# Nine sequence rows per partition, channel projection in the mode domain, and 8 KB weight runs in a linear-attention and spectral-mixing kernel

## The chip, the core and the metric

The kernel runs on one core of one Trainium2 chip. The metric is the device time of one execution in microseconds (us). Times are medians of three to seven executions. The profiler's span of one execution is about 2 us shorter than the time of the same execution.

Engine names as in the profile: PE multiplies matrices, PEld is its weight load, DVE is VectorE, ACT is ScalarE, POOL is GpSimd, SP only issues DMAs here. Casting loads (fp32 in memory, 16 bits on chip) are issued by POOL.

## The reference, cut to what matters

```python
# q, k, v: (8 batches, 8 heads, 576 rows, 64), w_r, w_i: (64 modes, 512, 512), w_ch: (512, 512), all fp32
phi = lambda x: np.where(x > 0, x, np.exp(x) - 1.0) + 1.0
kv  = einsum('bhsd,bhse->bhde', phi(k), v);  z = phi(k).sum(axis=2)
x   = einsum('bhsd,bhde->bhse', phi(q), kv) / (einsum('bhsd,bhd->bhs', phi(q), z)[..., None] + 1e-6)
x   = x.transpose(0, 2, 1, 3).reshape(8, 576, 512)
X   = rfft(x, axis=1)                       # only the first 64 modes are mixed
Yr  = Xr @ w_r - Xi @ w_i;  Yi = Xr @ w_i + Xi @ w_r      # per mode, 16 rows x 512 x 512
u   = x + irfft(Y, n=576)
out = u + maximum(u @ w_ch, 0)
```

The spectral weights are 128 matrices of 1 MB in fp32, 134 MB of the 164 MB that the kernel reads. Reading them cannot be avoided, so everything else should happen under it.

## The kernel before

Attention runs batch by batch. Seven weight buffers are filled while it runs. Then one mode after another is multiplied as its two matrices arrive. Results of four modes sit in four bands of 32 partitions, so a later stage has to bring them into one tile per batch. This is done by DMAs of 8 KB. The inverse DFT, the channel product and the output come last.

```python
def _w_load(kk):                                        # seven buffers; 2 KB runs: row (dc*128 + p) of the matrix
    wr = wpool.tile([128, NDC, D], BF16, tag="w", bufs=7)
    nc.gpsimd.dma_start(out=wr, in_=moe_w_r[kk].rearrange("(dc p) e -> p dc e", p=128))
    ...                                                 # the same for wi
for b in range(B):                                      # attention
    if b % 2 == 0: w_pref[b // 2] = _w_load(b // 2)
    for c in range(2):                                  # 512 B runs of q, k; 256 B runs of v; 64 tail rows apart
        nc.gpsimd.dma_start(out=q16[:, c], in_=q[b, :, c*256:(c+1)*256, :].rearrange("h (s2 par) d -> s2 h (par d)", par=2))
        ...
    ...
    nc.vector.tensor_copy(out=xt_c[:, :, 0, b, :], in_=xt_ps)       # DFT of x, transposed, modes contiguous
    ...
for g in range(NG):                                     # 16 groups of four modes
    for m in range(4):
        ...                                             # 4 matmuls with wr, 4 with wi, all into band mo = 32*m
    for m in range(4):
        nc.vector.tensor_copy(out=ystage[mo:mo+16, gg, :], in_=p1[mo:mo+16, :])
    if gg == HNG - 1:                                   # twice: 64 DMAs that reorder lanes into batches
        for b in range(B):
            for ri in range(2):
                for m in range(4):
                    nc.sync.dma_start(out=yg[b][k0+8*m : k0+8*m+8, ri, :], in_=ystage[lane : lane+1, :, :])
for b in range(B):                                      # output, per tile of 128 rows
    for j in range(NB + 1):
        ...                                             # 2 matmuls: inverse DFT; DVE: u = x + y
        nc.scalar.copy(out=u16, in_=u)                  # then 4 transposes, another ACT copy,
        ...                                             # 4 matmuls with w_ch, DVE: u + max(e, 0), store
```

## Time and profile before

The median is 594.36 us (592.34 to 595.3, 3 runs). The stages, as the chain of waits and the stretches below divide them:

| stretch, us | what | what sets its length |
|---|---|---|
| 0 to 174 | attention | 13 to 18 us from the DFT copies of one batch to those of the next, 16.3 on average (the 17.8 of the prediction fits two of these steps); no engine is full |
| 133 to 175, within it | DMA idle | seven buffers are full; the eighth load waits for the first product |
| 174 to 490 | weights | DMA: 2.54 us per 1 MB matrix, PE follows |
| 490 to 535 | reorder | SP issues 64 DMAs at 0.66 us each |
| 535 to 592 | rest of the output | PE 47 of 57 us |

The slice table of the kernel before: each column is 1/40 of the span (14.8 us). Digits are tenths of the time that the engine or the DMA engines were busy; PEclk is the granted PE clock in tenths; GB/s counts the bytes written, which for a casting load are half of those read.

```profile
PE   0378799999855665666666566766666654999885
PEclk9999999655556667666676766566767675857999
DMA  9999998992019999999999999999999990004444
GB/s 159 168 186 182 182 173 74 124 85 24 1 16 193 206 206 206 206 206 207 206 206 206 209 210 210 207 206 206 206 206 206 206 188 10 13 12 164 168 171 142
```

The row of DMA falls to 2, 0, 1 at 133 to 175 us. From there it is 9 in every slice at 206 GB/s until 490 us (206 to 210), then 0 for three slices (10 to 13 GB/s), then 4. The stretches, with the busy time of each engine in us (and its number of instructions), then granted clock, DMA share and GB/s:

```profile
core 0: us, PE busy (x) PEld busy (x) DVE busy (x) ACT busy (x) POOL busy (x), PEclk, DMA share, GB/s
40.00:174.00 134.00, 113.79 (x966) 71.84 (x967) 95.17 (x346) 76.00 (x120) 45.17 (x54) 0.75 1.04 99
174.00:490.00 316.00, 199.91 (x506) 54.27 (x503) 41.21 (x60) 0.00 (x0) 89.63 (x121) 0.66 1.22 203
490.00:535.00 45.00, 37.34 (x132) 11.18 (x130) 26.71 (x40) 11.87 (x21) 0.00 (x0) 0.65 0.07 12
535.00:592.00 57.00, 46.96 (x273) 20.62 (x272) 29.94 (x45) 30.06 (x59) 0.00 (x0) 0.95 0.48 167
```

Two pieces of the chain of waits of the kernel before (start in us, duration in us, what):

```profile
144.76 29.38 issue
174.15 5.37 DMA wi_1715<-in_moe_w_i_dram
179.52 17.86 DMA wi_2332<-in_moe_w_i_dram
...
493.63 0.71 DVE ystage_2740 L336
495.00 0.62 SPq L345
495.67 0.62 SPq L345
```

POOL issues nothing for 29.4 us because no buffer is free. In the list of waits it is this line (engine, line, releaser: us in total, times, longest):

```profile
POOL wi_1715 L120 <- PE P_0_2268 L317: 29.4, 1, 29.4
```

From 495 us on the chain is one SP issue of 0.62 us after the other, 0.66 us apart with the gap.

### The profile page before, as it was taken

The page shows a single profiled execution, that of the slowest core. Times are in us where ns is not written, and L with a number is a line of the kernel's source. Part 1 is how long each engine was busy: PE and PEld are TensorE (multiplying, and loading weights), DVE is VectorE, ACT ScalarE, POOL GpSimd, SP SyncE. Part 2 cuts the span into 40 slices and gives each one's busy share as a digit, 9 for nine tenths or more (in the row PEclk, how much of TensorE's full clock was granted, in tenths as well). Part 3 has the DMA queues.
Part 4 walks back from the last instruction along what each step waited for, and adds up shares of the span by engine and source line. Part 5 has one row for each costly group of instructions (what it writes and reads, how often), then busy time and mean ns, then how long its engine had stood idle before and what let it go on. Part 6 is the DMA issues. An engine that isn't in the chain of part 4 may idle for free.

```text
span 592.1 us, 5577 instructions
## 1 busy us (share of the span) xinstructions
PE 410.4 (69%) x1976; PEld 166.8 (28%) x1976; DVE 209.9 (35%) x529; ACT 131.7 (22%) x218; POOL 158.0 (27%) x205
## 2 busy tenths in 40 slices
PE   0378799999855665666666566766666654999885
PEld 0255465655521111111111111111111111323442
DVE  1486977877511101110110100311011103576653
ACT  1346666764420000000000000000000001602673
POOL 6656444430013323222323322223223200000000
PEclk9999999655556667666676766566767675857999
DMA  9999998992019999999999999999999990004444
GB/s 159 168 186 182 182 173 74 124 85 24 1 16 193 206 206 206 206 206 207 206 206 206 209 210 210 207 206 206 206 206 206 206 188 10 13 12 164 168 171 142
DMA packets 155243, 94.21 MB, mean 159 GB/s; under 512 B 83280, under 2 KB 150480, under 8 KB 155216
## 3 DMA queue, kind: packets, MB, share of 16 engines
q0 software_dynamic: 138896, 80.75, 96.0%
q1 hardware_dynamic: 16320, 13.12, 8.1%
q8 instruction: 15, 0.25, 0.2%
q14 instruction: 12, 0.10, 0.0%
HBM read 164.10 MB, written 9.44 MB: 293 GB/s over the span
## 4 chain that ended last, share of the span: by engine, by line
DMA 55%; PE 20%; issue 11%; SPq 7%; DVE 3%; ACT 2%; POOL 1%; DVEq 0%; POOLq 0%; ACTq 0%
SPq L345 7%; DMA wi_2332<-in_moe_w_i_dram 3%; DMA wr_2872<-in_moe_w_r_dram 3%; DMA wi_2821<-in_moe_w_i_dram 3%; DMA wi_2426<-in_moe_w_i_dram 3%; DMA wi_3009<-in_moe_w_i_dram 3%; DMA wi_2609<-in_moe_w_i_dram 3%; DMA wr_3060<-in_moe_w_r_dram 3%; DMA wr_2477<-in_moe_w_r_dram 3%; DMA wr_2660<-in_moe_w_r_dram 3%; DMA wi_2520<-in_moe_w_i_dram 3%; DMA wr_2966<-in_moe_w_r_dram 3%; DMA wi_2915<-in_moe_w_i_dram 3%; DMA wr_2571<-in_moe_w_r_dram 3%; DMA wi_3151<-in_moe_w_i_dram 3%
## 5 line engine op out<-in xcount | busy, mean ns | idle before, releaser
L370 ACT CAST u_0_0_3240<-x_main_76 128x512 f16<-128x512 f32 x1 | 0.6, 620 | 328.4 <-DVE x_main_76 L368 328.4
L326 PEld LDWEIGHTS <-xt_c 128*16 128x16 bf16 x256 | 32.3, 126 | 136.4 <-issue 132.2
L317 PEld LDWEIGHTS <-xt_c 128*16 128x16 bf16 x256 | 28.7, 117 | 127.9 <-issue 102.2
L336 DVE CAST ystage_2740<-P_8_2741 16x512 bf16<-16x512 f32 x4 | 2.7, 687 | 45.5 <-PE P_10_2847 L326 45.5
L219 PE MATMUL qT_0_146<-id_64,qp_128 128*64 128x128 f16 x8 | 1.3, 314 | 23.8 <-DVE qp_128 L179 23.8
L361 PEld LDWEIGHTS <-inv_sb 64*128 64x128 bf16 (+1 forms) x80 | 7.4, 111 | 28.0 <-issue 23.3
L219 PEld LDWEIGHTS <-qp_128 128*64 128x64 f16 x32 | 3.2, 158 | 25.3 <-DVE qp_128 L179 23.8
L336 DVE CAST ystage_2267<-P_1_2305 16x512 bf16<-16x512 f32 x4 | 2.7, 686 | 19.6 <-PE P_1_2305 L326 19.6
L336 DVE CAST ystage_2740<-P_13_3006 16x512 bf16<-16x512 f32 x4 | 2.7, 686 | 17.9 <-PE P_13_3006 L326 17.9
L336 DVE CAST ystage_2267<-P_7_2623 16x512 bf16<-16x512 f32 x4 | 2.7, 687 | 17.7 <-PE P_7_2623 L326 17.6
L336 DVE CAST ystage_2267<-P_3_2411 16x512 bf16<-16x512 f32 x4 | 2.8, 688 | 17.7 <-PE P_3_2411 L326 17.6
L336 DVE CAST ystage_2267<-P_5_2517 16x512 bf16<-16x512 f32 x4 | 2.7, 687 | 17.7 <-PE P_5_2517 L326 17.6
L336 DVE CAST ystage_2267<-P_6_2570 16x512 bf16<-16x512 f32 x4 | 2.7, 687 | 17.7 <-PE P_6_2570 L326 17.6
L336 DVE CAST ystage_2267<-P_2_2358 16x512 bf16<-16x512 f32 x4 | 2.7, 686 | 17.7 <-PE P_2_2358 L326 17.6
L336 DVE CAST ystage_2740<-P_15_3112 16x512 bf16<-16x512 f32 x4 | 2.8, 688 | 17.6 <-PE P_15_3112 L326 17.6
L336 DVE CAST ystage_2267<-P_4_2464 16x512 bf16<-16x512 f32 x4 | 2.7, 686 | 17.7 <-PE P_4_2464 L326 17.6
L336 DVE CAST ystage_2740<-P_14_3059 16x512 bf16<-16x512 f32 x4 | 2.7, 687 | 17.6 <-PE P_14_3059 L326 17.6
L336 DVE CAST ystage_2740<-P_11_2900 16x512 bf16<-16x512 f32 x4 | 2.7, 686 | 17.6 <-PE P_11_2900 L326 17.6
L336 DVE CAST ystage_2740<-P_12_2953 16x512 bf16<-16x512 f32 x4 | 2.7, 686 | 17.6 <-PE P_12_2953 L326 17.5
L120 POOL DMA_DIRECT2D wi_1715<-in_moe_w_i_dram x1 | 0.8, 756 | 29.4 <-PE P_0_2268 L317 29.4
L336 DVE CAST ystage_2267<-P_0_2268 16x512 bf16<-16x512 f32 x4 | 2.7, 686 | 9.8 <-PE P_0_2268 L326 9.7
L336 DVE CAST ystage_2740<-P_10_2847 16x512 bf16<-16x512 f32 x4 | 2.7, 687 | 9.5 <-PE P_10_2847 L326 9.5
(1543 smaller groups left out, 1070.2 us busy)
## 6 DMA issues: line engine op xcount, KB each, us to landing
wr_105<-in_moe_w_r_dram POOLq DMA_DIRECT2D x1, 512.0 KB, 7.3
wi_107<-in_moe_w_i_dram POOLq DMA_DIRECT2D x1, 512.0 KB, 9.8
q_0_109<-in_q_dram POOLq DMA_DIRECT2D x2, 256.0 KB, 11.8
k_0_110<-in_k_dram POOLq DMA_DIRECT2D x2, 256.0 KB, 12.9
v_0_111<-in_v_dram POOLq DMA_DIRECT2D x4, 128.0 KB, 11.8
q_1_375<-in_q_dram POOLq DMA_DIRECT2D x2, 256.0 KB, 9.3
k_1_376<-in_k_dram POOLq DMA_DIRECT2D x2, 256.0 KB, 9.7
v_1_377<-in_v_dram POOLq DMA_DIRECT2D x4, 128.0 KB, 9.1
```

Source lines behind the costliest of these rows:

```text
L120: nc.gpsimd.dma_start(out=wi, in_=moe_w_i[kk].rearrange("(dc p) e -> p dc e", p=128))
L219: nc.tensor.transpose(qT_ps[po : po + 64, j, :], q_p16[:, c, h, par, :], id16[:, :128])
L317: nc.tensor.matmul(p1[mo : mo + 16, :], xa[:, dc], wr[:, dc, :], start=(dc == 0), stop=False, tile_position=(0, mo),)
L326: nc.tensor.matmul(p1[mo : mo + 16, :], xb[:, dc], wi[:, dc, :], start=False, stop=(dc == NDC - 1), tile_position=(0, mo),)
L336: nc.vector.tensor_copy(out=ystage[mo : mo + 16, gg, :], in_=p1[mo : mo + 16, :])
L345: nc.sync.dma_start(out=yg[b][k0 + 8 * m : k0 + 8 * m + 8, ri, :], in_=ystage[lane : lane + 1, :, :],)
L361: nc.tensor.matmul(yps[:rows, :], inv_sb[:NM, ri, j * 128 : j * 128 + rows], yg[b][:, ri, :], start=(ri == 0), stop=(ri == 1),)
L370: nc.scalar.copy(out=u16[:rows, :], in_=u)
```

## The change

Its intent: (1) each partition takes nine consecutive rows of one head, so q, k and v arrive in runs of 9 x 64 x 4 = 2304 B with no tail rows; (2) the weights arrive with four consecutive matrix rows per partition, in runs of 8 KB; (3) 14 matrices instead of 7 can be loaded early; (4) the four 128-row parts of a product use four column groups of the PE, and their sum, together with the reordering, is done by a matmul with a 0/1 "pick" matrix, so the 128 small DMAs go; (5) u @ w_ch = x @ w_ch + irfft(Y @ w_ch): x @ w_ch is computed under the weight stream, Y @ w_ch on 16 rows per mode, and the output stage only adds.

```diff
-        nc.gpsimd.dma_start(out=wr, in_=moe_w_r[kk].rearrange("(dc p) e -> p dc e", p=128))   # 7 buffers
+            nc.gpsimd.dma_start(out=w, in_=src[kk].rearrange("(p dc) e -> p dc e", dc=NDC))    # 4 + 10 buffers
...
+            nc.gpsimd.dma_start(out=t, in_=src[b].rearrange("h s d -> (h s) d").rearrange(
+                    "(hp r j) d -> r hp (j d)", r=128, j=NJ))                # one load each for k, q, v
+        if b >= 1: ...                                                        # w_load(b - 1): two matrices per batch
...
-                    nc.vector.tensor_copy(out=xt_c[:, :, 0, b, :], in_=xt_ps)  # modes contiguous
+        nc.vector.tensor_copy(out=xt_v[:, :, :, 1, b], in_=xf[:, :, 0, :])     # 24 columns per mode: 48 B stride
+        nc.vector.tensor_copy(out=xt_v[:, :, :, 2, b], in_=xf[:, :, 1, :])
+        nc.scalar.mul(out=xt_v[:, :, :, 0, b], in_=xf[:, :, 1, :], mul=-1.0)
...
+            nc.tensor.matmul(P[quad, :], xt_c[:, dc, 8 + kk*SLOT : 8 + kk*SLOT + 32], wr[:, dc, :],
+                start=True, stop=False, tile_position=(0, dc * 32))             # quad = rows dc*32 .. dc*32+31
...                                                                             # the same with wi and stop=True
+            nc.tensor.matmul(yt_ps[:, ec, kk % 8, :], st[:, ec*128 : ec*128+128], pick_sb)
...
-                        nc.sync.dma_start(out=yg[b][...], in_=ystage[lane : lane + 1, :, :])   # 2 x 64 of them
+        if 4 <= kk < 52: ... channel_product(done)       # 36 tiles: x16, 4 transposes, copy, 4 matmuls, E0
+        if kk == NE - 1: ...                             # mode 55: z = Y @ w_ch and y = Y per batch, 112 of 128 rows
...
+    def finish(t, by_act):                               # output, 36 tiles
+        nc.tensor.matmul(e, id16, E0[t], ...); nc.tensor.matmul(y, inv, Y); nc.tensor.matmul(e, inv, Z, ...)
+        nc.vector.tensor_tensor(out=x, in0=x, in1=y, op=ALU.add)
+        if by_act:                                       # 16 tiles: relu on ACT, add on POOL
+            nc.scalar.activation(out=r, in_=e, func=AF.Relu)
+            nc.gpsimd.tensor_tensor(out=x, in0=x, in1=r, op=ALU.add)
+        else:                                            # 20 tiles: one DVE instruction
+            nc.vector.scalar_tensor_tensor(out=x, in0=e, scalar=0.0, in1=x, op0=ALU.max, op1=ALU.add)
```

## The prediction

> **What bounds it now.** The slice table and the chain of waits show four stages.
> (1) Attention, 0 to 174 us: about 17.8 us per batch (spacing of the DFT matmuls in the chain). No engine is full (18 us windows: PE 15.5, DVE 14, ACT 11).
> (2) At 133 to 175 us the DMA row falls to 2, 0, 1: seven weight buffers are full and the eighth load waits on the weight product (wi_1715, 29.4 us).
> (3) Weights, 175 to 490: the chain is nearly all weight DMA, DMA 9 of 9, 206 GB/s written as bf16, so 412 GB/s read as fp32; one 1 MB matrix per 2.54 us. PE (63%, clock 0.65) only follows.
> (4) 494 to 535: 64 small DMAs issued by SP at 0.66 us each, on the chain; then 57 us of output work with PE 47, DVE 30, ACT 30.
>
> **What the change does.**
> - Stage 4's 64 reorder DMAs vanish (PE picks rows instead; 8 small DMAs stay): about -38 us.
> - During attention 14 weight matrices can load instead of 7. So 114 remain after it: 114 x 2.54 = 290 us; before, 121.
> - 8 KB source runs instead of 2 KB. "DMA: Bandwidth & Descriptors" (Why small descriptors are slow) gives about 3 bus cycles per packet and (Measured) 425 GB/s at best, so at most 3%: estimate 2.47 to 2.54 us per matrix, 282 to 290 us.
> - q, k, v arrive in runs of 2304 B instead of 512 and 256 B, without 64-row tails. Estimate per batch from traced durations (DVE 0.40 per 128x256 multiply, 0.69 per 2048 fp16 scalar op; ACT 1.9 per 2048 exp): DVE 11, ACT 10.6, PE 10 to 12 us. DMA per batch (3.5 MB q,k,v plus 2.1 MB weights) at 412 GB/s: 13.7 us. So attention becomes DMA-paced at 13.5 to 14.5 us per batch, 44 MB by about 109 us; the last v lands then, with some 18 us of work behind it: attention ends near 128 us (118 to 145).
> - The channel product x@w_ch moves under the weight stream. Per mode PE gets 8 matmuls of 512 columns in four column groups, 4 picks, 0.75 channel product: under 3.5 us if the groups overlap ("TensorE: Matmul & The Clock Gate", Part 3), under the 5 us of DMA. All hidden.
> - Output stage: 36 tiles; 36 adds at 0.69 plus 20 relu-adds at 0.69 make DVE 39 us; 108 wide matmuls on PE about 27 to 40; 16 relus on ACT and adds on POOL. DVE-paced, 42 to 46 us.
>
> **Sum.** 128 attention + 4 restart (buffers full: DMA idles 15 to 20 us until mode 2 runs) + 286 stream + 8 last mode, z/y and small DMAs + 45 output = 471; about 2 more from span to time: 473 us. Range 452 to 502. Chances: faster 0.97, same 0.02, slower 0.01.
>
> **What would show it.** Slice table: DMA 9 over nearly all slices, with one gap of 15 to 20 us at the end of attention. Weight landings 2.47 to 2.54 us apart. In the stream, chain = weight DMA, PE under 75%. No SP issue row. Output stage DVE at 85% or more.
>
> **What would make it wrong.** Attention compute-paced (permuted fp16 views at half rate on DVE add 2.4 us per batch; shared PSUM slots stall PE): +15 to 25 us. The column groups not overlapping at a cold clock: PE 5.6 us per mode, stream PE-bound, +30 us. Output stage PE-paced at a half clock: +10 us. 8 KB runs bringing more than 3%: -10 us.

## The result and the profile after

The kernel after takes 487.6 us (486.92 to 488.39, 4 runs); the kernel before took 593.93 us in the same rounds. The ratio is 0.8214 (95% interval 0.819 to 0.8238). Ratios here are the mean time of one kernel's runs over that of the other's of the same rounds, so not quite the ratio of the medians quoted. All outputs were correct, in the experiments too. The time lies in the predicted range and is 14.6 us above the predicted 473.

The slice table of the kernel after (one column is 12.1 us):

```profile
PE   0344576556747675677675433232323359429870
PEclk9957655565557979988979755555555559757996
DMA  9999999990006999999999999999999999962995
GB/s 160 211 209 209 209 211 209 211 209 17 1 0 121 213 214 213 213 214 213 214 213 214 213 214 214 213 213 212 215 212 215 212 215 211 215 124 75 283 274 171
```

The DMAs are full from the start, at about 209 GB/s from the second slice on. Then there is one hole of three slices, and then mostly 213 to 214 GB/s until the last weight. The three slices of 10 to 13 GB/s near the end are gone. The stretches of the kernel after, with the same columns as before:

```profile
20.00:112.00 92.00, 50.61 (x656) 34.86 (x656) 67.73 (x146) 66.74 (x75) 20.00 (x29) 0.59 1.13 206
112.00:149.00 37.00, 21.85 (x240) 13.62 (x242) 18.86 (x41) 16.14 (x19) 0.14 (x1) 0.50 0.00 1
149.00:434.00 285.00, 146.49 (x1084) 65.39 (x1076) 44.02 (x82) 61.71 (x108) 60.42 (x114) 0.70 1.05 210
434.00:442.00 8.00, 5.88 (x23) 2.08 (x20) 1.36 (x3) 1.17 (x2) 0.00 (x0) 0.50 0.08 24
442.00:476.00 34.00, 26.50 (x111) 9.65 (x109) 33.51 (x56) 9.56 (x16) 20.18 (x16) 0.99 0.82 247
476.00:485.00 9.00, 0.00 (x0) 0.00 (x0) 0.00 (x0) 0.00 (x0) 0.00 (x0) 0.56 0.39 127
```

In 112 to 149 us the DMAs move nothing, although the last load of attention has landed and 114 weight matrices are still to come. The chain of waits across this hole:

```profile
97.15 0.35 POOL v_7_1362 L141
97.50 51.34 issue
148.86 0.51 POOL wr_1732 L119
...
160.50 19.13 DMA wr_1889<-in_moe_w_r_dram
```

and the wait of POOL behind it:

```profile
POOL wr_1732 L119 <- PE P_1627 L278: 51.0, 1, 51.0
```

v_7 is the last v. It was issued at 97.15 us and landed at 111.1 us. The next load is the first one that needs a freed weight buffer, and it is issued at 148.86 us. So nearly 38 us of work lay between the last landing and the freed buffer. How the time fell, from the chain and from the landings:

| from, to | before, us | after, us | saved |
|---|---|---|---|
| start to the first load that needs a freed buffer | 174.2 | 148.9 | 25.3 |
| to the landing of the last weight | 315.4 (121 matrices) | 285.0 (114 matrices) | 30.4 |
| to the end of the span | 102.6 | 51.4 | 51.2 |
| span | 592.1 | 485.2 | 106.9 |

Of the 30.4 us, seven fewer matrices at 2.61 us are 18.2, and 114 matrices at 0.107 us less are 12.2. (Here the whole stretch, its start included, is divided by the matrices: 315.4 / 121 = 2.61 and 285.0 / 114 = 2.50 us.)

The last 51.4 us hold a part that none of the stages above names. DVE ends at 475.65 us and the last store lands at 480.52. After that no DMA moves anything, and the trace has one long instruction left: a DRAIN on POOL (with which the program closes an engine), from 473.85 to 484.46 us. In the kernel before, POOL has nothing to do at the end, and its DRAIN (16.3 us) is over at 490 us.

### The profile page after: what moved, and what is told of

Its sections match the earlier page's. It is cut to its first block, busy times and chain, and to the rows that moved or that the text cites. A ratio compares the mean times of both kernels' runs of the same rounds, so it can differ in the third digit from the quotient of the medians.

```text
span 485.2 us, 5542 instructions
## 1 busy us (share of the span) xinstructions
PE 255.5 (53%) x2156; PEld 129.4 (27%) x2156; DVE 171.2 (35%) x337; ACT 163.5 (34%) x227; POOL 108.6 (22%) x173
## 4 chain that ended last, share of the span: by engine, by line
DMA 65%; issue 13%; DVE 8%; PE 7%; ACT 4%; POOL 0%; POOLq 0%; SPq 0%; DVEq 0%
DMA q_3_640<-in_q_dram 4%; DMA wi_3418<-in_moe_w_i_dram 4%; DMA wr_2621<-in_moe_w_r_dram 4%; DMA wr_3283<-in_moe_w_r_dram 4%; DMA wr_3109<-in_moe_w_r_dram 4%; DMA wr_2988<-in_moe_w_r_dram 4%; DMA wr_2865<-in_moe_w_r_dram 4%; DMA wr_2500<-in_moe_w_r_dram 4%; DMA wr_2256<-in_moe_w_r_dram 4%; DMA wr_2133<-in_moe_w_r_dram 4%; DMA wr_2012<-in_moe_w_r_dram 4%; DMA wr_2744<-in_moe_w_r_dram 4%; DMA wr_2377<-in_moe_w_r_dram 4%; DMA wr_1889<-in_moe_w_r_dram 4%; DMA k_5_998<-in_k_dram 4%
## 5 line engine op out<-in xcount | busy, mean ns | idle before, releaser
L284 PEld LDWEIGHTS <-xt_c 128*32 128x32 bf16 x248 | 11.8, 101 | 86.1 <-issue 84.9
L278 PEld LDWEIGHTS <-xt_c 128*32 128x32 bf16 x248 | 9.0, 98 | 44.9 <-issue 17.9
L182 PE MATMUL kvp_121<-vpad_100,ke_108 64*128 64x130 f16 x36 | 2.1, 308 | 15.2 <-DVE vpad_100 L171 15.2
L382 PEld LDWEIGHTS <-YT 128*112 128x112 f16 x32 | 7.7, 288 | 2.7 <-issue 2.2
L441 POOL TENSOR_TENSOR x_main_76<-x_main_76,r_3474 128x512 f32<-128x512 f32 x1 | 1.3, 1267 | 29.6 <-ACT r_3474 L440 29.6
L388 PEld LDWEIGHTS <-YT 128*112 128x112 f16 x32 | 7.5, 294 | 0.5
L182 PEld LDWEIGHTS <-ke_108 64*128 64x128 f16 x36 | 2.0, 141 | 15.1 <-DVE ke_108 L168 12.6
L424 PEld LDWEIGHTS <-inv_sb 128*128 128x128 f16 x32 | 3.2, 100 | 8.7 <-issue 6.6
L419 PEld LDWEIGHTS <-id_64 128*128 128x128 f16 x36 | 3.5, 100 | 6.4 <-issue 2.1
L423 PEld LDWEIGHTS <-inv_sb 128*128 128x128 f16 x32 | 3.3, 102 | 4.8 <-issue 1.7
L163 ACT ACTIVATE ke_108<-k_0_102 128x1152 f16<-128x1152 f16 x2 | 2.2, 1154 | 6.5 <-DMA k_0_102<-in_k_dram 6.5
L254 PE MATMUL xf_254<-fwd_sb,x_0_184 128*128 128x128 f16 x16 | 2.2, 263 | 4.0 <-ACT x_0_184 L248 4.0
L163 ACT ACTIVATE ke_468<-k_2_458 128x1152 f16<-128x1152 f16 x2 | 2.3, 1160 | 5.6 <-DMA k_2_458<-in_k_dram 5.6
L292 ACT CAST ys_3429<-P_3420 128x512 f16<-128x512 f32 x1 | 0.6, 586 | 10.4 <-PE P_3420 L284 10.4
L290 DVE CAST ys_3410<-P_3401 128x512 f16<-128x512 f32 x1 | 0.7, 691 | 9.4 <-PE P_3401 L284 9.4
L163 ACT ACTIVATE ke_828<-k_4_818 128x1152 f16<-128x1152 f16 x2 | 2.7, 1326 | 3.9 <-DMA k_4_818<-in_k_dram 3.9
L290 DVE CAST ys_2810<-P_2801 128x512 f16<-128x512 f32 x1 | 0.7, 692 | 9.1 <-PE P_2801 L284 9.1
L290 DVE CAST ys_3122<-P_3113 128x512 f16<-128x512 f32 x1 | 0.7, 691 | 9.1 <-PE P_3113 L284 9.1
L290 DVE CAST ys_2931<-P_2922 128x512 f16<-128x512 f32 x1 | 0.7, 692 | 9.1 <-PE P_2922 L284 9.1
L290 DVE CAST ys_2687<-P_2678 128x512 f16<-128x512 f32 x1 | 0.7, 691 | 9.1 <-PE P_2678 L284 9.1
## 6 DMA issues: line engine op xcount, KB each, us to landing
v_0_106<-in_v_dram POOLq DMA_DIRECT2D x1, 576.0 KB, 11.5
k_2_458<-in_k_dram POOLq DMA_DIRECT2D x1, 576.0 KB, 14.7
```

Of the source, the lines that this page charges most:

```text
L163: nc.scalar.activation(out=ev[:, c], in_=rv[:, c], func=AF.Exp)
L182: nc.tensor.matmul(kv_ps[:, h2, hpp * 130 : hpp * 130 + 130], kp[rows, hpp, j].rearrange("p o d -> p (o d)"), vp[rows, 2 * hpp : 2 * hpp + ...
L254: nc.tensor.matmul(o, x16[:, jj, dc::NDC], fwd_sb[:, jj, :], start=(jj == 0), stop=False)
L278: nc.tensor.matmul(P[quad, :], xt_c[:, dc, 8 + kk * SLOT : 8 + kk * SLOT + 32], wr[:, dc, :], start=True, stop=False, tile_position=(0, dc ...
L284: nc.tensor.matmul(P[quad, :], xt_c[:, dc, kk * SLOT : kk * SLOT + 32], wi[:, dc, :], start=False, stop=True, tile_position=(0, dc * 32),)
L290: nc.vector.tensor_copy(out=st, in_=P)
```

## The experiments

Twelve kernels were run. Two questions lead them: what sets the hole of 37 us and the pace of attention, and what each part of the change is worth.

| label | kernel and edit | us | ratio to before |
|---|---|---|---|
| e1_xt_layout | after, DFT result stored with contiguous modes | 480.41 | 0.8084 |
| e2_after_2k | after, weights in 2 KB runs | 495.29 | 0.8334 |
| e3_before_8k | before, weights in 8 KB runs | 583.47 | 0.9816 |
| e4_no_prefetch | after, no weight loads written between batches | 487.21 | 0.8201 |
| e4b_tied_late | after, all early weights held until the last v is in | 489.7 | 0.8252 |
| e5b_short_runs | after, q, k, v in 256 B runs, four loads each | 494.6 | 0.8336 |
| e5a_four_loads | after, four loads each, long runs | 482.01 | 0.8131 |
| e6_project_late | after, channel product back in the output stage | 510.26 | 0.859 |
| e8_before_twoq | before, reorder DMAs on SP and ACT | 585.99 | 0.9877 |
| e8b_before_poolq | before, reorder DMAs on SP and POOL | 579.35 | 0.9759 |
| e9_best | after, e1's layout and one early weight tied to each batch | 466.1 | 0.7857 |
| e10_balance | e9 with more output tiles on ACT and POOL | 476.46 | 0.8026 |

By the margin of 2% that the record uses, e8_before_twoq counts as the same as the kernel before (interval 0.9844 to 0.9910) and e3_before_8k as unclear (0.9784 to 0.9849). Both intervals lie below 1, so both are faster, but by little.

### e1_xt_layout: is it the strided copies?

One suspect for the hole was the three copies that store the DFT of a batch. Their instructions write 2-byte elements 48 B apart. The edit stores modes contiguously and lets the PE read its weights with a stride instead:

```diff
-        nc.vector.tensor_copy(out=xt_v[:, :, :, 1, b], in_=xf[:, :, 0, :])
+        nc.vector.tensor_copy(out=xt_v[:, :, 1, b, :], in_=xf[:, :, 0, :])
...
-                P[quad, :], xt_c[:, dc, 8 + kk * SLOT : 8 + kk * SLOT + 32], wr[:, dc, :],
+                P[quad, :], xt_c[:, x0[dc] + 8 : x0[dc] + 40, kk], wr[:, dc, :],
```

> The changed kernel with the spectral operand stored with the modes contiguous, so the three copies per batch that write it are dense again instead of 2-byte writes 48 bytes apart. Theory (attention is paced by its own chain of instructions, and these copies, 1.33 and 1.55 us on VectorE and 1.34 us on ScalarE where I had sized 0.31 to 0.37, stand in it): the copies fall to about 0.3 us, a batch in the loop gets 2 to 2.6 us shorter than 14.7, the first spectral product starts 9 to 14 us before 145 us, time 474 to 479 us. Rival (attention is paced by its loads until the last v lands at 111 us): only the work behind that load gets shorter, 4 to 7 us, time 480 to 484. Second rival (the copies are off the chain): 486 to 489.

It took 480.41 us (479.8 to 481.32), which is in the rival's range. Two of the DVE copies in the kernel after (busy us, mean ns | idle before), in its groups of instructions:

```profile
L261 DVE CAST xt_c<-xf_1514 128x256 bf16<-128x256 f32 x1 | 1.5, 1549 | 0.0
L260 DVE CAST xt_c<-xf_434 128x256 bf16<-128x256 f32 x1 | 1.3, 1334 | 2.3 <-PE xf_434 L257 2.3
```

and the copies of all eight batches in e1_xt_layout:

```profile
L258 DVE CAST xt_c<-xf 128x256 bf16<-128x256 f32 x8 | 3.4, 425 | 22.3 <-PE xf L255 18.2 <-PE kvp L180 4.1
L259 DVE CAST xt_c<-xf 128x256 bf16<-128x256 f32 x8 | 3.3, 415 | 0.0
```

The same 128x256 elements take 0.42 instead of 1.33 to 1.56 us on DVE, and 0.39 instead of 1.34 us on ACT. The batches did not come faster while loads were running: the DFT of the sixth batch was stored at 114.9 us against 114.7. Behind the last load they did: 11.5 and 11.6 us for the last two batches against 13.5 and 12.9, and the first load that needs a freed buffer was issued at 143.23 instead of 148.86 us. So the copies cost time only where no load sets the pace. The granted PE clock was 1.00 in attention in this profile and 0.59 in that of the kernel after. But e9_best below has the same 12.2 us between the first numerators (the attention outputs before the DFT) of its last two batches as e1_xt_layout, with a clock of 0.64 from 20 to 120 us. And the four executions of e1_xt_layout had mean clocks of 0.81, 0.82, 0.70 and 0.71 over the span, and all took 479.8 to 481.3 us. So the clock is not what shortened them.

"SBUF — State Buffer" of the Trainium skill (the note on cachelines, in Door 1: The DMA port swizzle) says that accesses pay when each one goes to a new 16-byte line. This case fits it for writes: 48 B apart, an element took three to four times as long. No other distance was tried, so that the lines are the reason is not shown. The price of the strided read that replaces it is on PEld, 155 to 158 ns per load of 32 columns against 98 to 100 ns with contiguous columns, and there it lies under the weight DMAs.

### e4_no_prefetch and e4b_tied_late: do the weight loads slow attention?

The rival: the 14 weight loads share the DMA engines with q, k and v and delay them. In e4_no_prefetch the loads between the batches were only left out of the loop:

```diff
-        if b >= 1:
+        if False:                                   # the loop behind attention loads all of them
```

> The changed kernel with no weight loaded between the batches: all fourteen early matrices are asked for after the last q, k, v. Theory (attention is paced by its own instructions, and its end leaves the DMA idle for 37 us): the fourteen matrices, 34 us of DMA, fit in the idle stretch at the end of attention, the first product stays near 145 us, time 484 to 492 us. Rival A (loads pace attention, weights among them take their turn): attention ends 8 us or more earlier, time under 480. Rival B (early loading is what saves the time): the stream gets the 34 us back, time 510 to 525 us.

It took 487.21 us, but it did not do what it was for. The order in which loads are issued is decided by the scheduler, and the first weight loads appeared in POOL's order at 27 us, among q, k and v. The run says nothing on the question. e4b_tied_late holds the loads back by data: each buffer first gets one element of the last v, so that its load cannot start earlier.

```diff
+            nc.vector.tensor_copy(out=w[0:1, 0, 0:1], in_=raw["v"][0:1, 0, 0:1])
+            nc.gpsimd.dma_start(out=w, in_=src[kk].rearrange("(p dc) e -> p dc e", dc=NDC))
```

> The changed kernel with the fourteen early weight matrices tied by a one-element copy to the last batch's v, so that the scheduler cannot put them among the q, k, v loads (which it did in the run before). Theory (loads pace attention until the last v lands, weights taking their turn in the queue): with the queue to themselves the batches follow at their own pace, 13.4 us as between the last two; the last batch's numerators start near 120 us instead of 133, the first spectral product near 131 instead of 145, the weights still fit before about 137, time 472 to 480 us. Rival (the engines' own chain paces attention): first product 142 to 146 us, the weights come after it, time 487 to 493 us.

It took 489.7 us (489.52 to 489.83), which is in the rival's range; the first product ran at 138.9 us, between what the two sides expected. Its GB/s row, in slices of 12.2 us:

```profile
GB/s 162 207 208 177 124 108 110 145 2 44 213 214 213 213 214 212 215 213 213 214 214 213 213 214 213 213 214 214 213 214 214 213 214 213 213 141 66 290 272 170
```

From the fourth slice on the DMAs carry q, k, v alone and are not full (108 to 177 GB/s). Still the first numerators of the batches come at 25.5, 40.0, 55.0, 69.7, 84.4, 99.1, 113.8 and 127.2 us, 14.5 to 15.0 us apart and the last 13.4. In the kernel after they come at 25.8, 44.5, 60.1, 76.0, 90.7, 105.3, 120.0 and 133.4 us, 14.6 to 15.9 us apart once running and the last 13.4. So the weight loads cost attention about 6 us, nearly all in the first batches. The engines' own chain of instructions, at 14.7 us, is as slow as that even where the DMAs are not full. And no engine is full there either: from 40.0 to 113.8 us, five batches, DVE is busy 56.6 us, ACT 53.9 and PE 48.4, that is 11.3, 10.8 and 9.7 us per batch of 14.75. The batch takes longer than its busiest engine needs, because the engines wait for one another. The first load that needs a freed buffer came at 142.69 us, but now the 14 early weights had to be read after attention, from 117.45 us on. The gain and the loss cancel: the last weight landed at 436.8 us against 433.8.

### e9_best: both limits at once

If two limits of nearly the same length hold attention, taking away either gains little and taking away both gains more. This kernel has e1's layout. It also ties one early weight to the v of each batch from the second on and eight to the last.

```diff
+    W_AFTER = (0, 1, 1, 1, 1, 1, 1, 8)
...
+        for _ in range(W_AFTER[b]):                # one-element copy from this batch's v, then the load
```

> Both together: dense spectral operand, and one weight matrix tied to the v of each of batches 1 to 6, eight to the last v. Theory (loads pace attention until 111 us, then the copies stand in the chain): batches every 11.5 us as between the last two of the dense run, first spectral product 118 to 126 us, DMA nearly without a gap, time 458 to 470 us. Rival (the two gains are the same gain): 473 to 480 us.

It took 466.1 us (465.61 to 467.15), 21.5 us less than the kernel after and the best of all. The batches come 12 to 14 us apart (numerators at 25.4, 39.3, 52.2, 65.4, 78.2, 90.9, 102.9, 115.1 us), the first load that needs a freed buffer at 127.93 us. Its slices (11.6 us each):

```profile
DMA  9999999927999999999999999999999999944985
GB/s 158 207 209 209 209 185 179 181 41 137 215 182 213 214 212 214 214 214 213 214 213 214 213 214 213 213 213 214 213 213 214 213 213 214 213 90 118 286 270 167
```

The hole has shrunk to about one slice at 41 GB/s and its neighbour at 137. e1's layout alone gained 7.2 us and tying alone, in the harsher form of e4b, lost 2.1 us. Together they gained 21.5, where independent costs would have given about 5. The two ties are not the same, so this is not a strict sum, but it is what two nearly equal limits give: shorter copies speed up the batches only when the loads are lighter, and lighter loads only when the copies are shorter.

### e2_after_2k and e3_before_8k: the 8 KB runs

```diff
-            nc.gpsimd.dma_start(out=w, in_=src[kk].rearrange("(p dc) e -> p dc e", dc=NDC))
+            nc.gpsimd.dma_start(out=w, in_=src[kk].rearrange("(dc p) e -> p dc e", p=128))
...
-                    o, x16[:, jj, dc::NDC], fwd_sb[:, jj, :], ...
+                    o, x16[:, jj, dc * 128 : dc * 128 + 128], fwd_sb[:, jj, :], ...
```

> The changed kernel with its weights read in 2 KB runs as before (512 weight rows spread as chunk, partition). Theory (the run length sets the rate of the stream): one matrix per about 2.54 us again instead of 2.457, 114 matrices, so 9 to 10 us longer: 496 to 498 us. Rival (the better rate comes from ten to fourteen buffers in place of seven, or from the other traffic): 486 to 490 us.

The other run puts 8 KB runs into the kernel before: the same edit the other way round, in its two loads and in the slice of the transpose.

> The kernel before with its weights read in 8 KB runs, nothing else changed. Theory (the run length sets the rate): 2.54 to 2.46 us per matrix over the 121 matrices that stream after attention, 9 to 11 us less: 583 to 586 us. Rival (seven buffers limit it): 592 to 595 us.

e2_after_2k took 495.29 us (494.73 to 496.15), 7.7 more than the kernel after and a little under what was expected, and e3_before_8k took 583.47 us (583.31 to 583.55), 10.4 less than the kernel before in the same rounds. The GB/s row of e2_after_2k:

```profile
GB/s 158 207 207 207 207 207 208 207 207 9 1 0 133 202 206 206 206 207 206 206 206 207 206 206 207 206 206 206 206 207 206 206 206 206 206 189 22 232 287 248
```

and that of e3_before_8k:

```profile
GB/s 165 168 189 187 181 172 78 119 73 45 6 1 185 213 213 214 212 213 214 213 213 214 215 217 218 213 215 213 212 215 213 212 157 11 13 12 165 181 163 144
```

With 2 KB runs both kernels write 206 GB/s in the stream, and with 8 KB runs both write 213 to 214, 3.6% more. So the runs are worth this by themselves, with few buffers too. The 7.7 us are less than the stream lost: the last weight landed 12.0 us later (445.8 against 433.8), but POOL's DRAIN took 2.1 us instead of 10.6 and did not delay the end, which gave 3.5 us back. Why that DRAIN is long in one kernel and short in the other was not tried. In terms of reads this is 412 against 427 GB/s. "DMA: Bandwidth & Descriptors" of the Trainium skill (Measured) has 425 GB/s for 16 MB, which agrees.

### e5b_short_runs and e5a_four_loads: the nine rows per partition

```diff
-            t = sA.tile([128, NHP, NJ * Dh], F16, tag="raw", bufs=5)
-            nc.gpsimd.dma_start(out=t, in_=... "(hp r j) d -> r hp (j d)" ...)
+            t = sA.tile([128, NHP, NJ, 66], F16, tag="raw", bufs=5)[:, :, :, 0:Dh]     # 256 B runs
+            for hp in range(NHP):
+                nc.gpsimd.dma_start(out=t[:, hp], in_=... "(r j) d -> r j d" ...)
```

> The changed kernel with q, k, v read in runs of 256 B (each row of 64 apart by a pad of two elements in SBUF, one load per head pair[...]). Theory (loads pace attention, and short runs slow them): 28.3 MB of q, k, v at two thirds of the rate or less, attention 12 to 25 us longer, time 499 to 512 us. Rival (run length matters little at this size, or attention is paced by its instructions): 486 to 491 us. A control with the four loads per tensor but long runs follows.

The control has the four loads per tensor and leaves the runs long ("(r j) d -> r (j d)").

> Control for the short-run kernel: the changed kernel with four loads per tensor and batch instead of one, runs still 2304 B. If the 7 us that the short-run kernel lost (494.6 against 487.6) came from the short runs, this one stays at 486 to 490 us with 205 to 211 GB/s in attention. Rival: the number of loads costs (72 more casting loads issued by GpSimd at roughly 1 us each): 492 to 496 us, and GpSimd as busy in attention as in the short-run kernel.

e5b_short_runs took 494.6 us, which alone looked like a loss of 7 us. But the control, e5a_four_loads, took 482.01 us (481.31 to 483.54), 5.6 less than the kernel after, which neither side had expected. So short runs cost 12.6 us by the right comparison. Of this 9.7 us are before the first load that needs a freed buffer (157.84 against 148.14 us). The pad that comes with the short runs also changes what the engines read; but the DVE and ACT instructions that read these tiles took 81.4 us in all against 79.6 in the control, so this rival explains 1.8 us at most. The packets of e5b_short_runs:

```profile
DMA packets 137195, 92.21 MB, mean 187 GB/s; under 512 B 115280, under 2 KB 116048, under 8 KB 137168
```

and of e5a_four_loads:

```profile
DMA packets 38891, 92.21 MB, mean 192 GB/s; under 512 B 4688, under 2 KB 17744, under 8 KB 38864
```

The bytes are the same in 3.5 times as many packets, and in attention, after the first slice, the DMAs write 139 to 184 GB/s instead of 204 to 209 in their slice tables. Why four loads are better than one is partly open. In e5a_four_loads the last v landed at 107.9 us instead of 111.1, with one weight load behind it, and the last DFT copy ended at 141.7 us instead of 145.0. But the first load that needs a freed buffer was issued at 148.14 us, hardly earlier than the 148.86 of the kernel after: by the list of waits it was held by a product that ran at 147.1 us, not by the third mode's at 144.7. The last weight lands 1.9 us earlier. The end, from that landing on, is 47.5 us instead of 51.4. Within it DVE needs the same time, and the last store lands 4.9 us after DVE's last instruction in both. The difference is POOL's DRAIN: it takes 2.8 us here and is over before the stores are, where in the kernel after it takes 10.6 us and ends 3.9 us after the last store. What makes it shorter was not tried.

### e6_project_late: the channel product under the stream

```diff
-        if 4 <= kk < 52: ...                        # x @ w_ch under the weight stream
+        if False:
...                                                  # no z; finish(): u16, 4 transposes, copy, 4 matmuls, max and add on DVE;
...                                                  # y and e have two PSUM buffers each instead of four; no work for POOL
```

> The changed kernel with the channel product done as before, on u in the output stage: no channel product under the weight stream, no z. Theory (the product is free under the stream and would stand in the output stage): the stream keeps 2.457 us per matrix, the output stage grows from 44 us to 58 to 64 (36 tiles at the 1.35 us per tile that the kernel before shows between its last tiles, or a little more), time 499 to 507 us. Rival (it costs the stream something): the stream gets shorter by 5 us or more, time under 497.

It took 510.26 us (508.31 to 511.04), 22.7 us more, somewhat beyond what was expected. The weight stream is as fast as with the projection in it: 210 GB/s from 149 to 434 us, as in the kernel after, although PE there is busy 98 us instead of 146. So the projection is free in the stream. In the output stage it is not. The two stretches, with the columns as before:

```profile
149.00:434.00 285.00, 97.57 (x768) 33.19 (x760) 29.49 (x46) 18.14 (x31) 59.88 (x114) 0.51 1.05 210
450.00:500.00 50.00, 42.18 (x260) 20.05 (x259) 35.62 (x57) 31.41 (x59) 0.00 (x0) 0.97 0.60 153
```

PE is busy 42 of 50 us, DVE 36 and ACT 31, and a tile needs all three in turn. The 22.7 us are a net figure: this output stage has fewer PSUM buffers, and as it gives POOL nothing to do, the kernel ends 1.2 us after its last store instead of 4.7.

### e8_before_twoq and e8b_before_poolq: the 64 reorder DMAs

The chain of the kernel before gives some 40 us to these issues. Is that what their removal gains?

```diff
-                        nc.sync.dma_start(
+                        (nc.sync, nc.scalar)[m % 2].dma_start(          # e8_before_twoq
+                        (nc.sync, nc.gpsimd)[m % 2 * wave].dma_start(   # e8b_before_poolq: second half only
```

> The kernel before with its 64 reorder DMAs issued in turn by the SP queue and the ACT queue, nothing else changed. Theory: the 0.62 to 0.66 us per DMA is the issue of one queue, so two queues halve the stretch of some 40 us: 573 to 580 us against 593.9, and the stretch between the last weight product and the first output matmul is 20 to 25 us. Rival: the stretch is not issue-bound (transfers or their landings pace it): 590 us or more.

> The kernel before with every second of its last 64 reorder DMAs issued by the POOL queue, which has nothing else to do by then, so that ACT stays free for the output stage (in the two-queue run with ACT, ACT could not begin its casts until 515 us, and the run gained 8 us instead of 14 to 20). Theory: the issue stretch halves to some 22 to 28 us and the output work, which overlaps it here, then sets the end: it took 68 us in that run when it began at 515, so begun at about 497 it ends near 565 to 572, a time of 566 to 576 us. Rival: the transfers, not the issue or ACT, were in the way: 582 us or more, as with the ACT queue.

In the timeline of e8_before_twoq (start, us, queue, what) the two queues share the 64 DMAs:

```profile
490.48 24.07 SPq L345 DMA_DIRECT2D yg<-ystage  x32
491.20 23.73 ACTq L345 DMA_DIRECT2D yg<-ystage  x32
```

The stretch fell from 43.5 us (492.2 to 535.6) to 24 us, as expected if one queue's issue is the limit; "DMA: Bandwidth & Descriptors" (Rules for kernel authors) says that spreading DMAs over engines only saves issue time, and this is that saving. But the kernel took 585.99 us (584.88 to 587.63), 7.0 less than before in the same rounds and not some 15 to 20. ACT was busy issuing until 515 us, and its casts for the output stage began only then. In e8b_before_poolq ACT is free, and the time is 579.35 us (577.64 to 581.37), 15.3 less than before in its rounds. That misses the expected 566 to 576 but is below the rival's 582. Its output stage:

```profile
494.00:520.00 26.00, 24.36 (x114) 9.51 (x115) 14.32 (x22) 13.66 (x25) 13.43 (x28) 0.77 0.32 90
520.00:530.00 10.00, 10.00 (x60) 4.09 (x57) 7.71 (x13) 5.23 (x11) 0.00 (x0) 1.00 0.44 157
530.00:540.00 10.00, 10.00 (x55) 3.86 (x54) 7.71 (x13) 6.17 (x12) 0.00 (x0) 1.00 0.45 153
```

PE is busy 44 of these 46 us. The issue is only halved here (21 us on SP), but PE stays this full until 570 us (73 of 76 us from 494 on), so its output work is the next limit. In the kernel before much of that work had run during the reorder (37 of 45 us). So removing the wait alone is worth about 15 us, not 38; taking away the second half of the issue as well was not tried, and PE leaves it some 3 us at most.

### e10_balance: can the output stage be shortened?

DVE paces the output stage, so one more tile in four was given to ACT and POOL in e9_best:

```diff
-            finish(b * NJJ + jj, jj % 2 == 1)
+            finish(b * NJJ + jj, jj >= 1)
```

> The best version so far (466.1 us) with three tiles of four per batch, instead of two, taking the relu on ACT and the last add on POOL; DVE has 8 fewer fused adds of about 0.69 us. Theory (output stage DVE-paced): 460 to 464 us, DVE still the busiest or level with POOL. Rival (stores or PE pace the output stage as much as DVE): 465 to 467 us; POOL slower than expected: above 467 us.

It took 476.46 us (474.43 to 477.83), 10.4 more than e9_best: the rival that POOL is slower than expected holds. In e9_best the middle of the output stage looks like this:

```profile
438.00:448.00 10.00, 8.85 (x36) 3.32 (x36) 10.00 (x17) 2.75 (x5) 5.36 (x5) 1.00 0.91 278
```

and in e10_balance, ten microseconds of it:

```profile
438.00:448.00 10.00, 7.56 (x31) 2.57 (x30) 8.92 (x15) 3.74 (x7) 6.80 (x6) 1.00 0.88 252
448.00:458.00 10.00, 4.87 (x16) 1.35 (x14) 3.29 (x6) 1.58 (x4) 6.55 (x6) 0.74 0.79 206
```

DVE falls from full to 8.9 of 10 us and then 3.3, while POOL goes on. POOL's last add ends at 462.4 us, where DVE had ended the stage at 454.2 in e9_best. An add takes POOL 1.27 us against DVE's 0.68 for its addition of the same size (one operand in PSUM), 1.87 times as long; "GPSIMD Engine Reference" of the Trainium skill (Performance versus the Vector engine) has 1.96 for a larger one. But 24 x 1.27 = 30 us of adds took 41 us (421.0 to 462.4), so POOL was also held up between them: by the list of waits, 10.1 of 11.6 us for the relu on ACT. The relu in turn waited for PE (16.5 us), for DVE (4.6) and for POOL's own adds (4.0). Which link of this ring sets the pace was not settled. After its last add POOL's DRAIN ends the kernel here too, 5.5 us after the last store.

## Why the prediction was right, and where it was off

The direction, the stages and the range were right. The profile after gives each term of the sum:

| term | predicted, us | measured, us | read from |
|---|---|---|---|
| attention | 128 (118 to 145) | 145.0 | last DFT copy ends |
| restart | 4 | 3.9 | to the issue at 148.86 |
| weight stream | 286 | 285.0 | to the last landing at 433.8 |
| last mode, z, y, small DMAs | 8 | 7.3 | to the first output matmul at 441.1 |
| output | 45 | 44.2 | to the end at 485.2 |
| span to time | 2 | 2.4 | 487.6, the median, less 485.2 (the profiled execution itself took 487.2) |

- **The mis-sized term is attention, in the step "the last v lands then, with some 18 us of work behind it".** The loads went as predicted: DMA full, the last v at 111.1 us instead of 109. But then 33.9 us of work followed, so that the hole in the DMA row was 37 us and not "15 to 20". The engines were about a batch and a half behind the loads. The copy of v_7 started only at 118.4 us, seven microseconds after the landing: until then DVE's timeline has the scaling of q_7, the DFT copies of the sixth batch and a minimum, with 2.3 us of waiting. The numerators of the seventh batch came at 120.0.
- **"Attention becomes DMA-paced" was half of it.** e4b_tied_late shows that the engines' chain takes 14.7 us per batch with the DMAs not full, as much as the loads and weights together. The predicted 13.5 to 14.5 was just missed (14.6 to 15.9 measured once running). The step that failed is the inference from busy time: the prediction took a batch to be as long as the larger of its DMA time (13.7 us) and its busiest engine (DVE, 11). In e4b_tied_late DVE is indeed busy 11.3 us per batch, yet the batches come 14.7 us apart. That attention could be compute-paced, at "+15 to 25 us", stood among the prediction's risks, and attention came out 17 us longer. The total is only 14.6 us off because the other terms were good, not because this one was. One part of the chain was sized wrongly: the copies of the DFT were taken at the 0.31 and 0.37 us that the contiguous ones have before, and took 1.33, 1.55 and 1.34 us. e1_xt_layout shows what this costs at the end (5.6 us earlier restart), and e9_best that it costs more where the loads are lighter.
- **"PE picks rows instead: about -38 us" is the right removal with the wrong price.** The SP issues are gone from the chain (SPq 0% of it). Taken alone they are worth some 15 us (e8b_before_poolq), because PE's output work was running beneath them. The end of the kernel nevertheless fell by 51.2 us, since moving the channel product takes another 22.7 us away (e6_project_late). The prediction's sum was built from the stages after, so this price did not enter it. The remaining 13 us of the 51.2 were not taken apart; POOL's DRAIN at the end works against the gain.
- **The weight stream was right.** 2.457 us per matrix between landings once running, a little better than "2.47 to 2.54": the rate rose by 3.6% (206 to 213.5 GB/s) where the prediction allowed "at most 3%". The two runs e2_after_2k and e3_before_8k show that the run length did it.
- **"All hidden" was right.** PE is busy 146 of 285 us in the stream, 51%, below the 75% named. The four column groups overlap: four matmuls of 512 columns end within 0.62 to 0.64 us at half clock, where four serial ones of about 0.63 us each took 1.81 to 1.87 us before. "TensorE: Matmul & The Clock Gate" (Part 3) describes this, and the trace agrees.
- **"DVE-paced, 42 to 46 us" was right in its pace and lucky in its number.** DVE is busy 33.5 of the 34 us from 442 to 476. But the prediction counted 56 DVE instructions at 0.69 us, 39 us in all, and they took 33.9: each record lasts 0.68 us, yet they start 0.60 us apart. What filled the rest was not named: 4.9 us until the last store has landed, and 4.7 us more until POOL's DRAIN and the closing of the program are over. The two errors cancel.

## What to carry to other kernels

When loads are tuned until they match the engines' own chain, the two limits hide each other: shorten both before judging either, and look for the moment the loads end, since there the depth of work behind the last one becomes idle DMA time. The busiest engine's time per batch is not the pace of a batch when the engines wait for one another: here it was 11.3 of 14.7 us. Look also past the last store: a DRAIN on POOL ended this kernel 4.7 us after it, and another with a shorter DRAIN 1.2 us after it. A share of the chain of waits is not what its removal gains (40 us of issue were worth about 15 here), because other work may be running beneath it and becomes the next limit. A control run that changes the shape of the loads without their run length was needed here to see the price of short runs at all.

## What the Trainium skill lacked or had wrong

- "VectorE: DVE Perf Modes" (Mode 1× (REGULAR) — the baseline) says that odd strides work at one result per cycle. Here a 128x256 copy from PSUM to bf16 took 0.42 us with contiguous writes and 1.33 to 1.56 us with writes 48 B apart. "SBUF — State Buffer" names the 16-byte lines that fit this, but gives no size of the penalty and does not say that it holds for ACT (0.39 against 1.34 us).
- "DMA: Bandwidth & Descriptors" has no rate of a casting load by run length. Measured on 0.5 MB written per load: 2 KB runs 412 GB/s read (206 written), 8 KB runs 427 (213 to 214). An estimate from its 3 cycles per packet at 32 B a cycle (Why small descriptors are slow) is (1 + 3/64) / (1 + 3/256), or 3.5% between the two, and the runs show 3.6%, so the estimate from the bytes read fits. Counted on the bytes written, half as many, it would be 6.9%, which the runs do not show.
- "DMA: Bandwidth & Descriptors" (Anatomy of one DMA) has some 50 ns of sequencer dispatch, for loads issued by GpSimd. For DMAs issued by SP or ACT the page has only a vendor's cycle count for "previous generations", and no page has a spacing measured on this chip. Here 8 KB DMAs followed each other at 0.66 us on SP alone and at 0.75 us on each of SP and ACT together, and while ACT issued its 32, none of its instructions ran.
- "TensorE: Matmul & The Clock Gate" (Part 1: The HAM clock gate) tells when the clock rises and falls, but not what a stage with PE busy about half the time gets. Two kernels with nearly the same PE work in attention (50.6 and 53.9 of 92 us busy) had 0.59 and 1.00 in their profiles, and four executions of the second one had 0.70 to 0.82 over their whole spans; no run here shows why.
- "GPSIMD Engine Reference" compares its add with DVE's at one size, 2048 elements with a ratio of 1.96. At 512 elements the ratio was 1.87 here (1.27 against 0.68 us, DVE's with one operand in PSUM), also while DVE and ACT worked beside it.
- No page has the DRAIN with which POOL closes its part of a program. It took 10.6 us in the kernel after and 2.1 to 12.1 us in the experiments that give POOL adds in the output stage; where it outlasted the stores, the kernel ended up to 5.5 us after the last one landed.
